# Two batches per unit, zero-padded 128-row matmuls and an MLP interleaved by hand in a sigmoid-attention kernel

## The chip, the cores and the metric

The kernel runs on one core of a Trainium2 chip. The metric is the device time of one execution in microseconds (us), as a median of several runs. Times of single stretches and instructions come from one profiled execution of each kernel. A run counts as slow when it lies over 1.5% above the fastest of the same kernel.

## The reference, cut to what matters

```python
# q, k, v: (8, 12, 448, 64) float32; w_q, w_k: (768, 64); w_out: (768, 768)
scores = q @ k^T / sqrt(64) - log(448)
attn   = 1 / (1 + exp(-scores))              # sigmoid, no row sums
x      = attn @ v                            # heads side by side: (8, 448, 768)
wq, wk = x @ w_q, x @ w_k
W_tok  = wq @ wk^T / sqrt(64)
out    = relu(W_tok @ x) @ w_out
```

There is no softmax, so score tiles are independent of each other. The mixing is computed as wq times (wk^T x), which keeps the inner size at 64.

## The kernel before

One batch at a time, a pair of heads at a time, in blocks of 112 rows (448 = 4 x 112).

```python
for b in range(B):                                     # 8 batches
    for hp in range(H // HPC):                         # 6 head pairs
        # load q, k, v in 256-byte runs, cast, transpose q and k  ... (cut)
        for hh in range(HPC):
            po = hh * HD
            for kb in range(NSB):                      # 4 blocks of 112 keys
                sco = psum.tile([SB, S], F32, tag="p")
                nc.tensor.matmul(sco, kT[po:po+HD, kb*SB:(kb+1)*SB],   # 64 rows of the array
                                 qT[po:po+HD, :], start=True, stop=True)
                attnT = work.tile([SB, S], BF16, tag="attnT")
                nc.scalar.activation(attnT, sco, Sigmoid, bias=bias_t[:SB], scale=attn_scale)
                nc.tensor.matmul(pxt[po:po+HD, :], vsb[:, kb, hh, :],  # 64 columns of the array
                                 attnT, start=(kb == 0), stop=(kb == NSB-1))
    # MLP of this batch, in blocks of 112 rows  ... (cut)
```

The order of the instructions is left to the scheduler. Weights are loaded whole, first of all.

## Time and profile before

| | before |
|---|---|
| median time | 499.0 us (498.6 to 499.98, 4 runs) |
| a batch: attention, MLP | 33.0 us, about 23 to 24 us |
| score tiles | 384 of 112 x 448 |
| mean granted TensorE clock | 0.94 |

In the profile, PE is TensorE (matmuls), PEld its weight loads, DVE VectorE, ACT ScalarE, POOL GpSimd and SPq the queue that issues DMAs; L404 is a line of the kernel. Matmuls write into PSUM, which the kernel's pools take in banks; SBUF is the working memory that the engines read from. The profile's page gives the busy time of each engine, the clock by slices, the chain of work that ended last, and groups of instructions with their mean duration and what ended the engine's idle time before them. The duration of a matmul includes time in the pipeline, in which the next one may already run. What a matmul costs in a stream is the distance between two starts. The prediction below shows the lines.

### The profile page before, as it was taken

How to read it: one execution, taken by the hardware profiler on the slowest of the kernel's cores; microseconds unless marked ns; L12 is line 12 of the kernel's file. 1: busy time of each engine (PE TensorE's matmuls, PEld its weight loads, DVE VectorE, ACT ScalarE, POOL GpSimd, SP SyncE). 2: the span in 40 equal slices, each digit the busy share in tenths (PEclk: the TensorE clock that was granted, in tenths of full speed). 3: DMA queues.
4: the chain of work that ended last, by engine and by line, in shares of the span. 5: the costliest groups of instructions: out<-in, count | busy, mean ns of one | idle time of the engine just before them, and what ended most of it. 6: DMA issues, size and time to landing. Idle time of an engine off the chain costs nothing.

```text
span 497.1 us, 6003 instructions
## 1 busy us (share of the span) xinstructions
PE 467.5 (94%) x2080; PEld 220.4 (44%) x2080; DVE 126.8 (26%) x363; ACT 348.0 (70%) x675; POOL 0.7 (0%) x7
## 2 busy tenths in 40 slices
PE   0699999999999999999999999999999999999986
PEld 0233344643446434643446434643446434553345
DVE  0121122043322431143221421233231432233100
ACT  1856555488856896488866896578865896578963
POOL 0000000000000000000000000000000000000000
PEclk9999999999979999699979999699979999699989
DMA  9634240365525441445325441345325452331003
GB/s 260 146 72 95 57 94 18 91 149 114 117 61 161 106 96 38 114 126 116 71 57 163 99 110 38 100 127 113 86 50 151 100 121 46 80 106 38 0 1 111
DMA packets 144206, 47.19 MB, mean 95 GB/s; under 512 B 136240, under 2 KB 143408, under 8 KB 144176
## 3 DMA queue, kind: packets, MB, share of 16 engines
q1 hardware_dynamic: 144176, 46.82, 38.7%
q8 instruction: 16, 0.26, 0.2%
q14 instruction: 14, 0.11, 0.1%
HBM read 35.78 MB, written 11.01 MB: 94 GB/s over the span
## 4 chain that ended last, share of the span: by engine, by line
PE 92%; ACT 3%; DMA 2%; issue 1%; DVE 0%; SPq 0%; ACTq 0%
PE sco L105 26%; PE pxt L116 25%; PE po L176 15%; PE ptr L94 7%; PE pt L128 6%; PE ptmp L156 4%; PE pm L165 4%; PE pwk L144 2%; DMA wo<-in_moe_w_out_dram 2%; PE pwq L135 2%; ACT x L131 1%; ACT xT L123 1%; ACT wout_sb L59 1%; DVE wk L149 0%; ACT L112 0%
## 5 line engine op out<-in xcount | busy, mean ns | idle before, releaser
L112 ACT ACTIVATE attnT<-sco,bias_t 112x448 bf16<-112x448 f32 x384 | 237.9, 634 | 38.9 <-PE pxt L116 36.1
L105 PE MATMUL sco<-qT,kT 64*112 64x448 bf16 x384 | 153.8, 417 | 1.7 <-ACT kT L98 1.5
L116 PE MATMUL pxt<-attnT,vsb 112*64 112x448 bf16 x384 | 152.2, 402 | 0.7 <-ACT attnT L112 0.7
L105 PEld LDWEIGHTS <-kT 64*112 64x112 bf16 x384 | 48.6, 130 | 80.4 <-issue 75.8
L176 PE MATMUL po<-wout_sb,mixT 128*112 128x384 bf16 x384 | 77.1, 370 | 0.0
L116 PEld LDWEIGHTS <-vsb 112*64 112x64 bf16 x384 | 40.8, 109 | 62.4 <-issue 50.7
L176 PEld LDWEIGHTS <-mixT 128*112 128x112 bf16 x384 | 57.1, 151 | 18.5 <-issue 0.7
L183 ACT COPY osb<-po 112x384 f32<-112x384 f32 x63 | 30.1, 478 | 46.9 <-PE po L176 38.3
L128 PE MATMUL pt<-ident,xT 128*112 128x128 bf16 x192 | 42.8, 260 | 7.4 <-ACT x L131 5.6
L131 ACT COPY x<-pt 112x128 bf16<-112x128 bf16 x119 | 28.4, 266 | 21.3 <-PE pt L128 15.8
L94 PE MATMUL ptr<-ident,qsb 112*128 112x112 bf16 x192 | 29.6, 249 | 14.2 <-DVE qsb L83 14.2
L123 DVE CAST xT<-pxt 128x448 bf16<-128x448 f32 x36 | 22.5, 625 | 77.4 <-PE pxt L116 77.4
L98 DVE COPY kT<-ptr 128x448 bf16<-128x448 bf16 x47 | 18.2, 387 | 85.8 <-PE ptr L94 85.8
L98 DVE COPY qT<-ptr 128x448 bf16<-128x448 bf16 x41 | 16.0, 391 | 68.6 <-PE ptr L94 48.0
L131 DVE COPY x<-pt 112x128 bf16<-112x128 bf16 x73 | 15.4, 223 | 68.2 <-PE pt L128 67.2
L128 PEld LDWEIGHTS <-xT 128*112 128x112 bf16 x192 | 21.7, 141 | 22.4 <-issue 15.5
L94 PEld LDWEIGHTS <-qsb 112*128 112x128 bf16 x192 | 15.3, 114 | 32.5 <-issue 16.8
L94 PE MATMUL ptr<-ident,ksb 112*128 112x112 bf16 x192 | 26.2, 238 | 0.8 <-DVE ksb L83 0.8
L167 ACT ACTIVATE mixT<-pm 128x448 bf16<-128x448 f32 x48 | 22.6, 546 | 5.7 <-PE pm L165 5.7
L156 PE MATMUL ptmp<-x,wk 112*64 112x384 bf16 x64 | 25.9, 404 | 0.3 <-DVE x L131 0.3
L83 DVE CAST vsb<-vsb 112x512 bf16<-112x512 f32 x47 | 19.7, 418 | 24.5 <-PE pxt L116 24.5
L94 PEld LDWEIGHTS <-ksb 112*128 112x128 bf16 x192 | 13.7, 107 | 20.1 <-issue 16.0
(33 smaller groups left out, 163.7 us busy)
## 6 DMA issues: line engine op xcount, KB each, us to landing
qsb<-in_q_dram SPq DMA_DIRECT2D x96, 112.0 KB, 2.7
ksb<-in_k_dram SPq DMA_DIRECT2D x96, 112.0 KB, 2.6
vsb<-in_v_dram SPq DMA_DIRECT2D x96, 112.0 KB, 2.4
out_dram<-osb SPq DMA_DIRECT2D x64, 168.0 KB, 2.2
wo<-in_moe_w_out_dram SPq DMA_DIRECT2D x1, 2304.0 KB, 11.3
wq<-in_moe_w_q_dram SPq DMA_DIRECT2D x1, 192.0 KB, 2.6
wk<-in_moe_w_k_dram SPq DMA_DIRECT2D x1, 192.0 KB, 2.9
```

The source lines that it names most:

```text
L94: nc.tensor.transpose(ptr[:, c * SB:(c + 1) * SB], src[:, c, :, :], ident16[:SB, :SB],)
L98: nc.any.tensor_copy(out=dst, in_=ptr)
L105: nc.tensor.matmul(sco, kT[po:po + HD, kb * SB:(kb + 1) * SB], qT[po:po + HD, :], start=True, stop=True,)
L112: nc.scalar.activation(attnT, sco, mybir.ActivationFunctionType.Sigmoid, bias=bias_t[:SB], scale=attn_scale,)
L116: nc.tensor.matmul(pxt[po:po + HD, :], vsb[:, kb, hh, :], attnT, start=(kb == 0), stop=(kb == NSB - 1),)
L123: nc.any.tensor_copy(out=xT_sb[hp], in_=pxt)
L128: nc.tensor.transpose(pt, xT_sb[c][:, si * SB:(si + 1) * SB], ident16[:DC, :DC])
L131: nc.any.tensor_copy(out=x_sb[si][:, c * DC:(c + 1) * DC], in_=pt)
L156: nc.tensor.matmul(ptmp, wk_s[si], x_sb[si][:, nb * 384:(nb + 1) * 384], start=(si == 0), stop=(si == NSB - 1),)
L167: nc.scalar.activation(mixT[c], pm, mybir.ActivationFunctionType.Relu, bias=0.0, scale=moe_scale,)
L176: nc.tensor.matmul(po, mixT[c][:, si * SB:(si + 1) * SB], wout_sb[:, c, nb * 384:(nb + 1) * 384], start=(c == 0), stop=(c == NDC - 1),)
L183: nc.any.tensor_copy(out=osb, in_=po)
```

## The change

The intent: fill the 128 x 128 array at every matmul, halve the number of sigmoids, stop waiting for weights at the start, and hide the MLP's TensorE work under the attention of the next two batches. The order of instructions on each engine is fixed by hand.

```diff
-    for b in range(B):
-        for hp in range(H // HPC):
+    NI, NP = 7, 64                      # 448 rows = 64 partitions x 7; two batches fill 128
+    kz = [singles.tile([P, NI, P], BF16, name=f"kz{n}") for n in range(NKZ)]       # zero-padded k
+    vz = [[singles.tile([P, NJ, NI, P], BF16, ...) for b in range(2)] for n in range(2)]
+    ps_s = pool("ps_s", 2, ...)         # scores: 2 buffers of 2 banks
+    ps_v = pool("ps_v", 2, ...)         # value accumulators: 2 banks
+    ps_f = pool("ps_f", 2, ...)         # q and k transposes and every MLP tile: 2 banks
+    ctx.enter_context(tc.manual_schedule())
...
+    for n, (u, j) in enumerate(pairs):  # 4 units x 6 head pairs
+        if n == 1:
+            load_weights()              # DMA and POOL casts of all weights, here
+        cast_qk(u1, j1); cast_v(u1, j1); tr = transposes(u1, j1)     # for the next pair
+        if j == 0 and u > 0:
+            fill = mlp(u - 1)
+            per_group = sum(c for c, _ in fill) / (NI * NJ - 2)
+        for gg in range(NI):            # a group: two score tiles
+            for slot in range(2):
+                nc.tensor.matmul(sc[:, slot, 0:S], kzt[u, j, b2][:, kblk, :], qt..., ...)
+            nc.scalar.activation(at, sc[:, :, 0:S], ACTF.Sigmoid, bias=bias_t, scale=attn_scale)
+            for _ in range(3):
+                if tr: tr.pop(0)[1]()   # 7 q transposes, then 7 k transposes
+            if len(pv_q) > LAG: flush_pv()              # value matmuls, two groups late
+            credit += per_group         # then MLP matmuls by an estimated cost
+            while fill and credit >= fill[0][0]:
+                cst, fn = fill.pop(0); credit -= cst; fn()
```

(An eviction is the copy of a PSUM tile to SBUF.) Loads now come in runs of up to 1792 bytes, and the casts from float32 are POOL's.

## The prediction

> **What bounds the kernel now.** I read the page's busy table first, then the clock row, the chain that ended last, the groups, and last two stretches of batch 2 (attention, then MLP) by engine and by instruction.
>
> ```profile
> PE 467.5 (94%) x2080; PEld 220.4 (44%) x2080; DVE 126.8 (26%) x363; ACT 348.0 (70%) x675; POOL 0.7 (0%) x7
> PEclk9999999999979999699979999699979999699989
> PE 92%; ACT 3%; DMA 2%; issue 1%; DVE 0%; SPq 0%; ACTq 0%
> L112 ACT ACTIVATE attnT<-sco,bias_t 112x448 bf16<-112x448 f32 x384 | 237.9, 634 | 38.9 <-PE pxt L116 36.1
> L105 PE MATMUL sco<-qT,kT 64*112 64x448 bf16 x384 | 153.8, 417 | 1.7 <-ACT kT L98 1.5
> L116 PE MATMUL pxt<-attnT,vsb 112*64 112x448 bf16 x384 | 152.2, 402 | 0.7 <-ACT attnT L112 0.7
> L176 PE MATMUL po<-wout_sb,mixT 128*112 128x384 bf16 x384 | 77.1, 370 | 0.0
> ```
>
> TensorE is 94% busy and 92% of the chain, so it sets the time, but busy is not streaming: a matmul's bar is longer than the distance to the next one. The stretches by engine (columns: stretch, length, busy time of PE, weight loads, DVE, ACT, POOL, then clock, DMA share, GB/s) give the period of a batch:
>
> ```profile
> 155.56:188.59 33.03, 33.03 (x137) 13.33 (x138) 12.16 (x33) 29.76 (x49) 0.00 (x0) 1.00 0.47 110
> 188.59:212.56 23.97, 22.95 (x126) 13.85 (x124) 4.07 (x13) 12.53 (x35) 0.00 (x0) 0.79 0.31 81
> ```
>
> A batch is 33.0 us of attention at full clock and about 23 to 24 us of MLP at a lower one (0.79 here, 0.85 in the next batch): 57 us, eight times, plus about 19 us before the first sigmoid and a slow first batch. The timeline of TensorE inside attention shows why attention costs 33 us:
>
> ```profile
> 163.34 0.39 PE L105 MATMUL sco<-qT,kT 64*112 64x448 bf16 x1
> 163.66 0.38 PE L116 MATMUL pxt<-attnT,vsb 112*64 112x448 bf16 x1
> 163.97 0.39 PE L105 MATMUL sco<-qT,kT 64*112 64x448 bf16 x1
> 164.29 0.38 PE L116 MATMUL pxt<-attnT,vsb 112*64 112x448 bf16 x1
> ```
>
> A 64-row score matmul and a 64-column value matmul alternate, and each start is 0.31 to 0.32 us after the last. Matmuls of one full-array shape do much better: consecutive starts of the output matmuls (L176, N=384) lie 0.162 us apart. So a score tile costs TensorE 0.63 us, and 48 tiles 30 us. ACT looks bound too (a 0.634 us sigmoid in a 0.63 us period), but right at the start, where score tiles had queued up behind the table load, five sigmoids take 2.95 us:
>
> ```profile
> 19.44 2.95 ACT L112 ACTIVATE attnT<-sco,bias_t 112x448 bf16<-112x448 f32 x5
> ```
>
> They include a wait; the first four start 0.53, 0.52 and 0.52 us apart. ACT can do a tile in 0.52 us; TensorE can't.
>
> **What the Trainium skill says.** (1) "TensorE: Matmul & The Clock Gate", section "Back-to-back issue gap": warm, N/2.4 + 2.5 ns. That is 162.5 ns at N=384, and the trace has 162; it gives 189 ns at N=448, and the trace has 189 between the wq matmuls (L135, 128 rows by 64 columns, one after another). (2) "TensorEngine Tiling (Array Packing)", section "Key Properties": changing the tiling mode drains the engine. The 0.31 us against 0.189 us above agrees. (3) "Advanced Engine Details and Errata", section "The Read-Write Bubble": each ACT or DVE instruction pays a fixed latency, so use large tiles; several PSUM banks may be read at once. The trace agrees on the fixed part: ACT's copies of 128 and 384 elements take 266 and 478 ns, 0.83 ns an element, so 0.52 us for 448 is 373 ns of elements and some 143 ns fixed. (4) "VectorE: DVE Perf Modes", section "Zero memsets can be issued as uint32 (trn2)": a memset takes a cycle per element whatever the type. No instruction of the kernel before shows it.
>
> **The change part by part.** There are now four units of two batches, six head pairs each, seven groups a pair. A group is two score matmuls, one sigmoid over 2x448, two value matmuls, two transposes on average and a share of the previous unit's MLP.
>
> *Attention on TensorE.* 336 score tiles of 128 rows for 384 of 112, all 128x128 on the array, so no mode switch: 4 x 189 = 756 ns a group, and 14 transposes a pair at 56 ns (128 columns by (1)), 112 a group: 868 ns. For the two batches that is 42 x 0.868 = 36.5 us; it was 66.
>
> *ACT.* By the fixed part of (3) a 2x448 sigmoid should start 143 + 747 = 890 ns after the last: 42 a unit are 37.4 us, plus 12 Relu of 448 at 440 ns (their distance in the trace), 5.3: 43 us a unit. No bound except in unit 0, which has no MLP to fill with.
>
> *MLP.* Per unit 24 matmuls of 448, 98 of 384 and 49 transposes: 4.5 + 15.9 + 2.7 = 23.2 us; it was 2 x 23 to 24. It sits between the attention matmuls at full clock. Streaming sum of a unit with filling: 36.5 + 23.2 = 59.7 us.
>
> *DVE.* A bf16 eviction of 448 takes 391 ns (448/1.92 + 158) but the next starts after 309; fp32 takes 625. A pair: q 625, k in eight pieces about 1.9 us, two value evictions 1.25; a unit with MLP about 40 us. Not a bound, but its queue is in order.
>
> *POOL.* Casts of 2560 elements a pair. From the small POOL rows (a memset of 128 takes 204 ns and of 1 takes 99; the select 292) 0.8 to 1.5 ns each, so some 2 to 4 us and overheads. Hidden under a 6 to 14 us pair.
>
> *Stalls that the hand order adds.* Two PSUM banks (ps_f) serve the q and k transposes and every MLP tile. TensorE is in order. While a transpose tile is open (groups 0 to 4 of 7) the MLP has one bank, so when one MLP tile ends and the next begins within a group, TensorE waits for the tail of the matmul (0.215 us past its stream), DVE (0.558) and two semaphore hops (0.04 + 0.05): **0.87 us**. Going through the written order of a unit, I count per pair: the first k transpose directly after the last q one (also 0.87, while an MLP tile holds the other bank); one or two mid-group boundaries of output tiles; and one tile that must wait behind the eight k evictions (0.4 to 1.5). This is 3.0, 4.2 and 3.2 us in pairs 3 to 5, 1.3 in pair 0, 7.0 in pair 1 (six x transposes a tile). In pair 2 the mix tiles are one matmul each and go through ACT's Relu (about 0.85 us a tile): 7.9. Sum **26.6 us a unit**. Some will overlap or be given back, so I take three quarters: 20. A filled unit is 59.7 + 20 = 80 us.
>
> *Start.* q and k no longer wait for the 2.3 MB weight. But DVE clears 26,880 bf16 columns before its first eviction: 28 us at a cycle each, 14 if issued as uint32. First sigmoid at 18 or 32 us; weight casts may hold up pair 1 somewhat. I take 25.
>
> *Tail.* The last MLP stands alone: 2.3 us of wq/wk, x transposes at DVE's pace with the clock falling (6.5), 3.5, mix at 0.51 us a tile (6.3), output 14.5, last eviction and store 4, the last value group 1: 38 us.
>
> Sum: start 25 + unit 0 at about 0.92 us a group (the first four groups of a pair have three transposes, 924 ns, the rest are ACT's 890) 39 + 3 x 80 + tail 38 = 342. The bank waits are the softest term and I counted them pessimistically, so I settle at **332 us**, 0.67 of before.
>
> **The rivals.** *A: no bank stalls.* If evictions keep pace, a filled unit is 60 to 62 us and the total 275 to 285. For it: an eviction is shorter than a six-matmul tile. Against it: two banks, three kinds of tile, in-order TensorE. *B: stalls in full, and the memset at one cycle per 2-byte element*: 32 + 40 + 3 x 87 + 40 = 373. *C: POOL is the bound.* At 3 ns an element with overheads a pair is 8.5 us, above unit 0's 6.4 but below a filled pair: some 13 us more, about 345. *D: ACT's sigmoid doesn't overlap with the next* (1007 ns a group): unit 0 becomes 43, the filled units stay as they are: 336. *E: the padding buys nothing* and full matmuls still cost 0.31 us: attention alone is 42 x 4 x 0.31 = 52 us a unit and the total near 400; the 0.162 and 0.189 us spacings speak against it. None reaches 499.
>
> **Range and chances.** A and B are the two ends, hence 285 to 375. Faster by over 2%: 0.97; within 2%: 0.02; slower: 0.01, for something like a POOL cast several times slower than its rows suggest.
>
> **What would show it.** Score and value matmuls 0.19 us apart within a group: the mode switch is gone. Sigmoids of about 1.0 us, 0.89 to 0.95 us apart in unit 0. A clock near 1.0 until the tail. Idle or waiting time of TensorE at the first k transpose, the x transposes, the mix and the output tiles, released by DVE evictions or the Relu, of 15 to 27 us a unit: right; under 5 us: rival A. The first sigmoid's time tells the memset. The prediction is wrong if POOL's casts release the transposes in the filled units, or if spacing within a group stays near 0.31 us.

## The result, and the profile after

| | before | after |
|---|---|---|
| median time | 499.0 us | 379.25 us (376.41 to 379.62, 4 runs) |
| ratio | | 0.7588, 95% interval 0.7562 to 0.7615 |
| span of the profiled run | 497.1 us | 377.2 us |

A ratio is the mean time of one kernel's fast runs over that of the other's of the same rounds, so it is not quite the ratio of the medians. The change is a clear gain. The time lies above the predicted 332 us and 4 us outside the range of 285 to 375.

The page of the changed kernel (the rows of busy time, clock, DMA, the chain by engine, then groups as in the prediction: count, busy us, mean ns, idle before and its releaser):

```profile
PE 276.6 (73%) x1692; PEld 149.8 (40%) x1692; DVE 161.6 (43%) x391; ACT 189.3 (50%) x217; POOL 88.4 (23%) x177
...
PEclk9995599999579999999999999999958999999989
DMA  8995999990000137839940039728960011232046
...
PE 55%; DVE 19%; DMA 7%; ACT 6%; SPq 6%; issue 4%; POOL 2%; POOLq 0%
...
L409 ACT ACTIVATE at<-sc,bias_t 128x896 bf16<-128x896 f32 x168 | 164.8, 1009 | 128.5 <-PE sc L404 110.4
L404 PE MATMUL sc<-qt,kz 128*128 128x448 bf16 x336 | 96.7, 371 | 7.6 <-DVE kz L182 6.3
L359 PE MATMUL pv<-at,vz 128*128 128x448 bf16 x336 | 95.5, 368 | 0.0
L271 PE MATMUL po<-wout,mx 128*128 128x384 bf16 x336 | 70.7, 332 | 17.5 <-DVE o L277 10.6
```

TensorE fell from 94% busy to 73% and from 92% of the chain to 55%; DVE (19%), DMA and others have entered it. No engine is busy throughout, which is how a kernel looks that waits. The clock row drops to 5 in three places. The duration of a score matmul hardly changed (417 to 371 ns), so the gain must be looked for in the distance of starts. The timeline of TensorE in unit 0, which has no MLP to interleave (columns: start, length, line, operation, count):

```profile
57.63 0.54 PE L404 MATMUL sc<-qt,kz 128*128 128x448 bf16 x2
58.01 0.33 PE L164 MATMUL ptr<-ident,q 128*128 128x128 bf16 x3
58.18 0.54 PE L359 MATMUL pv<-at,vz 128*128 128x448 bf16 x2
58.55 0.54 PE L404 MATMUL sc<-qt,kz 128*128 128x448 bf16 x2
```

Two score matmuls take 0.38 us of the stream (57.63 to 58.01), three transposes 0.17, two value matmuls 0.37. That is 0.19 us a matmul, where the kernel before needed 0.31 to 0.32. A group lasts 0.92 us here. The sigmoids of 896 elements start 0.89 to 0.92 us apart.

Now the stretches by engine. The rows are unit 0 (from its first sigmoid), units 1, 2 and 3 (3 up to the last sigmoid), and the tail:

```profile
core 0: us, PE busy (x) PEld busy (x) DVE busy (x) ACT busy (x) POOL busy (x), PEclk, DMA share, GB/s
18.20:76.60 58.40, 40.13 (x246) 21.72 (x245) 21.25 (x65) 38.46 (x44) 29.71 (x56) 0.85 0.97 231
76.60:167.60 91.00, 70.18 (x424) 37.77 (x423) 37.40 (x95) 47.83 (x56) 17.16 (x34) 0.92 0.34 82
167.60:254.10 86.50, 65.05 (x426) 35.58 (x423) 37.52 (x96) 47.89 (x55) 20.25 (x40) 1.00 0.52 128
254.10:338.90 84.80, 67.04 (x399) 35.91 (x396) 34.04 (x85) 46.92 (x54) 12.23 (x24) 0.92 0.38 92
338.90:377.20 38.30, 29.92 (x184) 16.24 (x181) 17.29 (x32) 6.93 (x13) 0.00 (x0) 0.96 0.36 91
```

Two batches of attention with an MLP take 84.8 to 91 us where they took 2 x 57 before, though DVE is busy for 34 to 38 us and ACT for 47 of them. Against the sum in the prediction:

| part | predicted | measured |
|---|---|---|
| start, to the first sigmoid | 25 (18 or 32) | 18.2 |
| unit 0 | 39 | 58.4 |
| units 1 to 3 | 240 | 91.0 + 86.5 + 84.8 = 262.3 |
| tail | 38 | 38.3 |
| sum | 342, recorded as 332 | 377.2 |

Three places explain the difference. The first is one pair in unit 0. In the next fence the rows are pairs 1 and 2 of unit 0, then pair 1 of units 1 and 2:

```profile
25.90:51.10 25.20, 8.38 (x46) 4.52 (x47) 3.76 (x12) 6.54 (x8) 15.58 (x28) 0.66 0.90 226
51.10:57.40 6.30, 6.30 (x44) 3.51 (x42) 3.61 (x11) 6.30 (x8) 3.03 (x6) 1.00 1.15 216
87.40:108.60 21.20, 16.22 (x93) 9.00 (x91) 8.21 (x20) 7.05 (x7) 3.03 (x6) 0.68 0.00 1
178.80:195.00 16.20, 10.60 (x89) 6.55 (x88) 8.21 (x20) 7.05 (x7) 6.25 (x13) 1.00 0.84 203
```

Pair 1 of unit 0 lasts 25.2 us, its neighbour 6.3. POOL's timeline tells why (in brackets: idle time before and what ended it):

```profile
27.98 0.51 POOL L333 CAST wqk<-wq 128x384 bf16<-128x384 f32 x1 [10.94 <-DMA wq<-in_moe_w_q_dram]
...
34.09 0.83 POOL L339 CAST wout<-w 128x768 bf16<-128x768 f32 x1 [2.31 <-DMA w<-in_moe_w_out_dram]
...
40.96 0.83 POOL L339 CAST wout<-w 128x768 bf16<-128x768 f32 x1 [2.05 <-DMA w<-in_moe_w_out_dram]
41.73 0.93 POOL L127 CAST q<-q 128x896 bf16<-128x896 f32 x1
```

POOL runs its queue in order. The weight casts stand in it ahead of the q cast of pair 2 and wait for their transfers, which stand behind those of four pairs in a DMA queue that is 0.90 busy over this stretch. The q cast, whose data had long landed, starts at 41.73 us, and TensorE waits 17.0 us for it at once (the longest wait of its transposes for POOL).

The second place is the filled units. The list of waits names what TensorE waited for (total us, times, longest):

```profile
PE pm L259 <- ACT mx L264: 14.1, 23, 0.9
...
PE po L271 <- DVE o L277: 10.6, 14, 1.0
...
PE px L223 <- DVE xn L228: 8.0, 13, 0.7
PE ptr L164 <- DVE qt L171: 7.2, 10, 0.7
```

These are the four costliest of the kinds of tile that share the two banks of `ps_f`: mix, output, x transposes, and k behind q. One such wait in the timeline of pair 3 of unit 2:

```profile
218.68 0.49 PE L271 MATMUL po<-wout,mx 128*128 128x384 bf16 x2
219.21 0.56 DVE L277 COPY o<-po 128x384 f32<-128x384 f32 x1 [2.48 <-PE po L271]
219.82 0.48 PE L271 MATMUL po<-wout,mx 128*128 128x384 bf16 x2 [0.65 <-DVE o L277]
```

The second of the two matmuls at 218.68 starts 0.16 later and ends its stream at about 219.0. The next tile's first matmul, of the same group, starts at 219.82. In between lie the tail of the matmul, an eviction of 0.56 and the hops: about 0.8 us with nothing on TensorE. To add all of them up I took the distance of each two starts on TensorE, less N/2.4 + 2.5 ns at the granted clock, wherever it is more than 0.06 us over. In unit 2, by pair, against the count in the prediction:

| pair | 0 | 1 | 2 | 3 | 4 | 5 | unit |
|---|---|---|---|---|---|---|---|
| counted, us | 1.3 | 7.0 | 7.9 | 3.0 | 4.2 | 3.2 | 26.6 |
| measured, us | 2.0 | 6.9 | 7.0 | 2.9 | 4.4 | 3.5 | 26.7 |

The third place is the clock. Pair 1 of unit 1 ran at 0.68 and took 21.2 us, pair 1 of unit 2 at 1.00 and took 16.2, with the same TensorE work and nearly the same waits (6.2 and 6.9 us). In units 1 and 3 the clock was at half for 13.7 us, in unit 2 never.

### The profile page after: what moved, and what is told of

Same layout as the page of the kernel before. It is cut to its first block, busy times and chain, and to the rows that moved or that the text cites. A ratio compares the mean times of both kernels' runs of the same rounds, so it can differ in the third digit from the quotient of the medians.

```text
span 377.2 us, 4927 instructions
## 1 busy us (share of the span) xinstructions
PE 276.6 (73%) x1692; PEld 149.8 (40%) x1692; DVE 161.6 (43%) x391; ACT 189.3 (50%) x217; POOL 88.4 (23%) x177
## 4 chain that ended last, share of the span: by engine, by line
PE 55%; DVE 19%; DMA 7%; ACT 6%; SPq 6%; issue 4%; POOL 2%; POOLq 0%
PE sc L404 14%; PE pv L359 13%; PE po L271 13%; DVE kz L182 5%; PE ptr L164 5%; ACT mx L264 4%; PE px L223 3%; DMA k<-in_k_dram 3%; PE pt L247 3%; SPq L100 3%; DVE xt L364 2%; PE pm L259 2%; DVE o L277 2%; PE pw L208 2%; DVE xn L228 2%
## 5 line engine op out<-in xcount | busy, mean ns | idle before, releaser
L409 ACT ACTIVATE at<-sc,bias_t 128x896 bf16<-128x896 f32 x168 | 164.8, 1009 | 128.5 <-PE sc L404 110.4
L404 PE MATMUL sc<-qt,kz 128*128 128x448 bf16 x336 | 96.7, 371 | 7.6 <-DVE kz L182 6.3
L359 PE MATMUL pv<-at,vz 128*128 128x448 bf16 x336 | 95.5, 368 | 0.0
L271 PE MATMUL po<-wout,mx 128*128 128x384 bf16 x336 | 70.7, 332 | 17.5 <-DVE o L277 10.6
L364 DVE CAST xt<-pv 128x448 bf16<-128x448 f32 x48 | 30.0, 624 | 64.4 <-PE pv L359 64.1
L182 DVE COPY kz<-ptr 64x384 bf16<-64x384 bf16 x96 | 34.1, 355 | 42.7 <-PE ptr L164 40.3
L277 DVE COPY o<-po 128x384 f32<-128x384 f32 x56 | 31.1, 556 | 48.0 <-PE po L271 44.2
L271 PEld LDWEIGHTS <-mx 128*128 128x128 bf16 x336 | 32.9, 99 | 46.5 <-issue 13.5
L404 PEld LDWEIGHTS <-kz 128*128 128x128 bf16 x336 | 33.1, 101 | 45.4 <-issue 17.9
L138 POOL CAST vz<-v 128x192 bf16<-128x192 f32 x96 | 29.4, 346 | 1.9 <-DMA v<-in_v_dram 1.5
```

What stands on the lines that cost most here:

```text
L138: nc.gpsimd.tensor_copy(out=z[:, j, 3 * hh : 3 * hh + 3, 64 * hh : 64 * hh + 64], in_=t[:, hh].rearrange("p (m d) -> p m d", m=3),)
L182: nc.vector.tensor_copy(out=z[r, 3 * hh : 3 * hh + 3].rearrange("p m (r n) -> p r m n", r=2), in_=ps[r, 0:6, b2].rearrange("p (r m) n -> p ...
L271: nc.tensor.matmul(st["po"], st["mx"][c][:, i * P : (i + 1) * P], wout16[:, c, nb * NB : (nb + 1) * NB], start=(c == 0), stop=(c == NC - 1),)
L277: nc.vector.tensor_copy(out=st["o"][:, nb * NB : (nb + 1) * NB], in_=st["po"])
L359: nc.tensor.matmul(ps, vz[u % 2][b2][:, j, (blk // 2 + 3 * (blk % 2)) if blk < 6 else 6, :], at[:, slot, :], start=(blk == 0), stop=(blk = ...
L364: nc.vector.tensor_copy(out=xts[u][j][:, :, b2, :], in_=ps)
```

## The experiments

All gave correct results. The first four ran on one chip in one set of rounds, the next four in another, the last two in a third; the kernel before took 498.1, 499.2 and 498.6 us there. The changed kernel itself had 379.25 us.

**Weights spread over the pairs.**

```diff
-        if n == 1:
-            load_weights()
         ...
             cast_v(u1, j1)
             tr = transposes(u1, j1)
+        weights_cast(n)    # n == 2: wq, wk; n == 2..4: two chunks of w_out each
+        weights_dma(n)     # n == 1: wq, wk; n == 1..3: two chunks of w_out each
```

> Only the weights move: two chunks a pair, cast behind the pair's own casts, in place of all of them ahead of pair 2's casts. My theory: pair 1 of unit 0 took 25.2 us in place of 6.3 only because POOL, in order, held the q cast of pair 2 behind weight casts that waited for a saturated DMA queue. It expects pair 1 near 7 us, unit 0 near 40 us and a total of 379 - 18 = 361 us (357 to 365). Rival: the first 80 us are bound by the DMA bandwidth itself (0.99 busy), so the same bytes cost the same time wherever they stand: pair 1 gets short, but later pairs of unit 0 get longer, total 374 or more.

Measured: 356.8 us (351.34 to 365.01, 4 runs); two of the runs count as slow, the fast two took 351.34 and 356.03. Pair 1 of unit 0 took 6.3 us and unit 0 39.6:

```profile
26.00:32.30 6.30, 6.30 (x44) 3.52 (x43) 3.62 (x11) 6.30 (x9) 5.00 (x11) 1.00 1.14 283
18.20:57.80 39.60, 38.15 (x241) 20.65 (x239) 21.14 (x65) 38.27 (x43) 24.50 (x45) 1.00 1.09 254
```

All weights were cast by 49 us, between the pairs' own casts, and no later pair of unit 0 became longer than 6.6 us. The theory stands and the bandwidth rival falls: 58.4 - 39.6 = 18.8 us were lost to where the weights stood in the queues. (The edit moves the weights' transfers and their casts together; the two were not tried apart.) The fast runs lie just under the expected 357 to 365 us: in the profiled one the clock was at half in one filled unit in place of two. The last experiment returns to the spread between runs.

**The MLP in one piece, nothing interleaved.**

```diff
-            fill = mlp(u - 1)
-            per_group = sum(c for c, _ in fill) / (NI * NJ - 2)
+            while pv_q:
+                flush_pv()
+            for _, f in mlp(u - 1):
+                f()
```

> The MLP of a unit runs in one piece ahead of the next unit's attention, nothing interleaved. My theory: two PSUM banks make the interleaving cost about as much as it hides. Attention alone is 42 groups of 0.9 us = 38 us (as in unit 0), the MLP alone about 33 us (as in the tail), with the restart some 72.5 us a unit, against 86 to 91 interleaved: total about 333 us (325 to 345). Rival: interleaving does hide work, as it was meant to, and taking it away makes each of three units longer: 380 us or more.

Measured: 321.39 us (319.75 to 324.08, 4 runs). Taking the interleaving away made the kernel 58 us faster. The theory was right in direction and too cautious by 12 us. The two rows are the last pair of unit 0 with the MLP behind it, and the first pair of attention after that:

```profile
69.40:106.80 37.40, 33.26 (x218) 18.61 (x217) 19.60 (x41) 12.35 (x20) 3.03 (x6) 1.00 0.23 57
106.80:113.10 6.30, 5.86 (x42) 3.21 (x39) 3.24 (x11) 6.26 (x8) 0.35 (x1) 1.00 0.89 236
```

The MLP alone takes 37.4 - 6.3 = 31.1 us and six pairs of attention 37.8, so 68.9 us a unit against 84.8 to 91 interleaved. In one piece the MLP has both banks, and the waits of a unit add up to 9.3 us by the measure above.

**One whole MLP tile a group.**

```diff
-                credit += per_group
-                while fill and credit >= fill[0][0]:
-                    cst, fn = fill.pop(0)
-                    credit -= cst
-                    fn()
+                for fn in fill.pop(0)[1]:   # fill now lists tiles: 38 for 40 groups
+                    fn()
```

> The MLP is cut at tile ends: one whole tile a group (38 tiles, 40 groups), so that the attention matmuls of a group stand between two tiles. Same instructions, same banks. My theory: the 26.6 us a filled unit are waits for a bank between two MLP tiles in one group; most of them go, what stays is the first k transpose (about 5 us a unit) and waits behind the k evictions (2 to 3 us), and the mix groups become ACT's (3.6 us more). A filled unit near 71 us, total about 329 us (320 to 342). Rival: the evictions on DVE are the limit whatever the order, so the waits move but stay: 365 us or more.

Measured: 316.05 us (314.52 to 317.01, 4 runs), below the expected band. The waits of a filled unit fell from 26.7 to 8.1 us and the unit to 68.0 (unit 2, where the changed kernel took 86.5 at the same clock):

```profile
144.70:212.70 68.00, 62.77 (x425) 35.45 (x424) 37.00 (x95) 46.00 (x56) 20.30 (x40) 1.00 0.63 163
```

The DVE rival falls: every eviction is still there and takes as long. The mix groups did not become as long as I had feared (I had added 3.6 us), and the clock stayed at 1.0 in all filled units.

**A third bank for the filling pool.**

```diff
-    ps_v = pool("ps_v", 2, space=bass.MemoryType.PSUM)
-    ps_f = pool("ps_f", 2, space=bass.MemoryType.PSUM)
+    ps_v = pool("ps_v", 1, space=bass.MemoryType.PSUM)
+    ps_f = pool("ps_f", 3, space=bass.MemoryType.PSUM)
```

> A bank goes from the value accumulators (2 to 1) to the filling pool (2 to 3), order unchanged. My theory: about 20 of the 26.6 us a filled unit go; each pair pays 0.9 us where the second batch's accumulation begins right behind the first one's (about 5.5 us a unit, and 5 to 8 in unit 0, which has no slack). Total about 342 us (330 to 358), waits at the first value matmul released by the DVE eviction of the value accumulator. Rival: the number of banks in the filling pool is not what TensorE waits for; then only the cost shows: 395 us or more.

Measured: 343.37 us (342.54 to 345.33, 4 runs). In the list of waits a new first entry for TensorE stands, the price foretold:

```profile
PE pv L359 <- DVE xt L364: 37.9, 31, 2.0
```

The waits for the filling pool fell from 26.7 to about 5 us a unit (mix 3.3, k transposes 1.4, x 0.5), and the value accumulators added 10.4, more than the 5.5 that I had estimated. Without touching the order, the number of banks alone moves the waits. That is the direct proof of what TensorE waited for. That the total met the estimate is in part luck: the price was higher than estimated, in unit 0 too (67.6 us for 58.4), and the clock, at half for only 3.4 us in the filled units against 27 in the changed kernel, gave some 9 us back.

**k transposes later, on top of one tile a group.**

```diff
             for _ in range(3):
-                if tr:
+                if tr and (gg >= 3 or len(tr) > NI):
                     tr.pop(0)[1]()
```

> The one-tile-a-group kernel (316 us), and the seven k transposes start in group 3 in place of right behind the last q transpose. My theory: the first k transpose waits for the bank that q's eviction frees; in the one-tile kernel the starts of transposes lag 2.7 us a filled unit behind the stream. Most of that goes: 310 us (306 to 313). Rival: the k evictions now end too late for the next pair's first scores, and each of 23 pairs pays for it: 320 us or more.

Measured: 308.4 us (307.99 to 308.73, 4 runs). The starts of transposes now lag 0.4 us a filled unit in place of 2.7, and a unit takes 65.5 us. The first scores of a pair still find their k in time. The theory stands.

**Score matmuls without the padding of k.**

```diff
+                r = slice(0, P) if blk == 6 else slice(64 * (blk % 2), 64 * (blk % 2) + 64)
                 nc.tensor.matmul(
-                    sc[:, slot, 0:S], kzt[u, j, b2][:, kblk, :],
-                    qt[u, j][:, b2].rearrange("p i n -> p (i n)"), start=True, stop=True,
+                    sc[:, slot, 0:S], kzt[u, j, b2][r, kblk, :],
+                    qt[u, j][r, b2].rearrange("p i n -> p (i n)"), start=True, stop=True,
```

> The changed kernel, but six of seven score matmuls of a batch take only the 64 rows that hold data (no zero padding of k in use); their two row halves alternate. My theory: going from 64 rows to 128 and back drains the array, 0.126 us each time as in the kernel before (0.315 against 0.189 us a start), so a group costs 0.25 us more, a pair of unit 0 goes from 6.3 to 7.8 or 8 us and the total to about 420 us (405 to 430). Rival: the two halves run side by side on different rows, the second starting some ns after the first, which pays for the drains: pair of unit 0 6.3 to 6.7 us, total 376 to 390.

Measured: 394.05 us (389.12 to 398.86, 4 runs); two of the runs count as slow (mean clock 0.887), the fast two took 389.12 and 389.72. By these the total lies inside the rival's band and below mine. The timeline of TensorE in unit 0 shows what happens inside a group:

```profile
60.44 0.36 PE L405 MATMUL sc<-qt,kz 64*128 64x448 bf16 x2
60.74 0.29 PE L164 MATMUL ptr<-ident,k 128*128 128x128 bf16 x2
60.86 0.54 PE L359 MATMUL pv<-at,vz 128*128 128x448 bf16 x2
```

Two score matmuls on different row halves together last 0.36 us, no longer than one alone: their starts in the trace are 0.003 us apart. The first of them starts 0.285 us after the value matmul ahead of it, in place of 0.189, and the next full-array instruction 0.29 after them. So the pair costs about 0.39 us where two padded ones cost 0.38. The rival is right about the mechanism, and about the pairs of unit 0 (6.6 us, against 6.3). Unit 2, at full clock in both kernels, takes 89.2 us against 86.5. At 0.3 us in the pairs of unit 0 and 2.7 in each of three filled units, padding k is worth some 10 us, which is what the fast runs differ by (389 and 379).

The traces also show what the change of mode costs. In a stream of full-array matmuls, the weights of the next one load while the one before runs: in the changed kernel a weight load starts at 57.633 us for the matmul that starts at 57.820. At a change they load only with their own matmul (60.438 and 60.442 here, and so for the alternating score and value matmuls of the kernel before). In that kernel the starts lie 0.118 us over 0.189 (medians) after a value matmul and 0.134 after a score matmul, whose own weight loads take 0.106 and 0.123 us. So its 0.31 us is close to a weight load and a stream one after the other. What holds the load back is not shown.

**One sigmoid per score tile.**

```diff
-            nc.scalar.activation(at, sc[:, :, 0:S], ACTF.Sigmoid, bias=bias_t, scale=attn_scale)
+            for slot in range(2):
+                nc.scalar.activation(at[:, slot], sc[:, slot, 0:S], ACTF.Sigmoid,
+                                     bias=bias_t, scale=attn_scale)
```

> The changed kernel with one sigmoid per score tile (448) in place of one per two (896). My theory: an activation pays 0.14 us whatever its size, so a group of unit 0 takes 1.03 us of ACT in place of 0.90 and a pair 7.2 us in place of 6.3; the filled units stay, TensorE sets them; total about 384 us (380 to 390). Rival: ACT never limits and the finer grain starts value matmuls sooner: no change or less, pairs of unit 0 at 6.3 us or below.

Measured: 378.63 us (376.76 to 384.14, 4 runs; the run of 384.14 counts as slow, the fast three took 376.76 to 378.76). In unit 0 a pair took 7.2 to 7.5 us in place of 6.3 to 6.6, as the theory said: sigmoids start 0.516 us apart, two of them 1.03 us. The total doesn't tell, because the profiled run lost half clock for 17 us where the changed kernel's had lost 27 us in its filled units. The double sigmoid is worth about 1 us in each pair in which ACT sets the pace, and no worth is seen in the filled units (13.0, 14.4 and 14.3 us in pairs 3 to 5 of unit 1, as in the changed kernel).

**The three repairs together.** Spread weights, one tile a group, late k transposes.

> Weights spread over pairs, one MLP tile a group, late k transposes, together. My theory: the gains add, as they lie in different stretches: 316 - 18.5 - 6 = 291 us (286 to 298), unit 0 at 39 us, filled units at 66 us, tail 37. Rival: with unit 0 fast, its loads and those of unit 1 meet a saturated DMA queue and unit 1 gives part of it back: 303 us or more.

Measured: 292.16 us (291.22 to 292.75, 4 runs), ratio to the kernel before 0.5849 (0.5832 to 0.5867). The gains add. This version beats both kernels. Its page, and a filled unit (unit 2):

```profile
PE 257.9 (89%) x1692; PEld 143.6 (49%) x1692; DVE 159.9 (55%) x391; ACT 182.9 (63%) x217; POOL 89.1 (31%) x177
...
PEclk9999999999999999999999999999999999999799
```

```profile
123.70:189.30 65.60, 62.69 (x426) 35.27 (x424) 36.97 (x97) 45.80 (x56) 20.30 (x40) 1.00 0.68 169
```

TensorE is busy for 62.7 of 65.6 us, with 59.7 us of streaming. The clock row has no dip before the tail.

**The MLP in one piece, with spread weights.** The edits of the first two experiments together.

> MLP in one piece and weights spread, no interleaving. What is interleaving worth once its waits are cut? My theory: 321 us less the 18.5 us of the weight hold: 303 us (299 to 307), so well-cut interleaving (292 us) is worth about 10 us over none, far from the 23 us of MLP streaming a unit that it was to hide, because TensorE streams 60 us a unit either way and only the idle time is at stake. Rival: with the pairs at ACT's pace and no slack, loads run late without the MLP's pauses, total 310 us or more.

Measured: 303.99 us (302.72 to 307.1, 4 runs). Well-cut interleaving is worth 304 - 292 = 12 us over none. (The 292 us kernel also has the late k transposes and this one has not; but the waits of most pairs without filling add up to 0.2 us here, so they can explain little of it.) Loads did not run late (no pair of attention over 6.6 us except the first, 8.6).

**x transposes cut at tile ends, with spread weights.**

```diff
                 credit += per_group
+                done = 0
                 while fill and credit >= fill[0][0]:
-                    cst, fn = fill.pop(0)
+                    if fill[0][2] and done:       # an x tile would begin here
+                        credit = 0.0
+                        break
+                    cst, fn, _ = fill.pop(0)
                     credit -= cst
+                    done += 1
                     fn()
```

> The kernel with spread weights, and of the MLP only the x transposes are cut at tile ends (no x tile begins in a group that has already done filling work). Four runs of the spread-weights kernel lay between 351 and 365 us, and its profiled run had TensorE's clock at half for 14 us in the x phase of one of three units, which made that pair 20.8 in place of 16.5 us. My theory: the bank waits in the x phase leave TensorE so idle that the clock falls in some units of some runs; with about 3 us of waits a unit gone it stays up: 343 us (338 to 348), spread between runs under 4 us, clock 1.0 in every unit's x phase. Rival: the transposes as such let the clock fall, not the waits: the spread stays near 10 us and some x phases still show half clock.

Measured: 329.9 us (328.52 to 330.6, 5 runs), a spread of 2 us, and clock 1.0 in all x phases of the profiled run. Of the spread that the run was to explain, 351 to 365 us, the upper two runs count as slow. The fast two lie 4.7 us apart, about what one stretch of half clock costs (20.8 against 16.5 us in pair 1), and their mean clocks agree with that: 0.994 and 0.975, where all five runs here have 0.994 to 0.999. The rival, that transposes as such let the clock fall, is weakened: the same transposes ran at clock 1.0 here, and in the profiled runs of the MLP in one piece, where they stand closer still. It is not excluded: other runs of the latter with spread weights have mean clocks down to 0.982, and where the clock fell in them is not on record. The time is 13 us better than I expected. Setting the credit to zero also moved later tile ends: all waits of a filled unit fell to about 20 us, not only those of the x tiles. So the run shows that the clock stays up when the filling is cut differently; how idle TensorE has to be for it to fall stays open.

## Why the prediction was wrong

Its direction and most of its steps held, and the time came out 47 us above it. In the order of its working:

- **What bounds the kernel before** held. The start distance in attention went from 0.31 to 0.19 us with full-array matmuls. The experiment without k's padding qualifies the reason: a change of mode costs about 0.1 us, with a weight load that no longer overlaps, and two row halves side by side can pay for it. In the kernel before, a 64-row and a 64-column matmul alternated singly, so every start paid. How much of the 0.31 us is due to the value matmul's 64 columns was not tried.
- **The spacing formula**, point (1) from the skill, held: 0.189 us at 448 columns, 0.162 at 384, 0.056 at 128. But that section gives the formula for an isolated matmul and says that a stream with weight loads has other spacings (about 81 ns at N=128, 131 at N=512), which the prediction left out. The trace decides for the formula at 128, and its 448 columns already take longer than those 131 ns; 512 was not run.
- **ACT** held: 0.89 to 0.92 us a sigmoid, unit 0 at 6.3 us a pair, and one sigmoid per tile cost what the fixed part says. Rival D (1007 ns a group) falls with it.
- **Start**: 18.2 us, the lower of the two cases. The memsets are issued as uint32 (2688 elements for 5376). I had taken 25 because I could not tell, and to cover the weight casts.
- **"weight casts may hold up pair 1 somewhat"** is the first step that failed. The mechanism was seen and its size was not worked out: 18.9 us in pair 1, against at most 7 in the sum. The parts were there: six chunks, two buffers, each waiting for a transfer behind four pairs of prefetched loads, and an in-order POOL.
- **The count of the bank waits** held to 0.1 us a unit and to 1 us in each pair.
- **"Some will overlap or be given back, so I take three quarters"** is the step that failed most. Nothing was given back: of the 26.6 us counted, 26.7 stand between the starts of unit 2, at full clock, so each wait of the engine that sets the time was paid in full. The discount took 6.6 us from each of three units, and settling on 332 below the own sum of 342 took 10 more.
- **Clock near 1.0 until the tail** failed too. Units 1 and 3 each lost some 5 us in pair 1 (21.2 and 21.1 against 16.2 us). Why there and not in unit 2 stays open.
- **Tail** held: 38.3 us for 38. Its parts are off by up to 1.2 us in both directions, and the clock fell at the start of the output matmuls (357.0 to 360.4 us), not in the x transposes.

Rival B had the stalls right with 3 x 87 us, and its memset wrong; that its 373 us come so near is luck, as 14 us of a memset that did not happen stand in for the weight casts. Rival C, POOL's rate, was not the bound (a q cast takes 0.94 us), but POOL's order was. A and E fell. The difference to the record, 377.2 - 332 = 45 us by the span, is made of -7 at the start, +19 in unit 0, +22 in the filled units and +10 of the last rounding down.

Where did the rest of the expected gain go? Interleaving was to hide some 23 us of MLP streaming a unit. It cannot, as TensorE streams both: 59.7 us a unit whichever way. Only the idle time beside it can be won, 9.3 us a unit when the MLP stands alone, and cutting by estimated cost spent 27 us of waits to win it.

## What to carry to other kernels

When work is interleaved by hand on an in-order engine, cut it where its buffers change hands: two kernels with the same instructions and banks differ by 63 us (379 and 316), some 10 of them through the clock, and what was changed is only where a group's share of that work ends. Before putting a queue's rare work (weight casts) ahead of its regular work, count what it waits for, because everything behind it waits too. And a wait that has been counted on the path that sets the end should be left at full size in the sum, unless a reason for a discount can be named.

## What the Trainium skill lacked or had wrong

- "TensorEngine Tiling (Array Packing)", section "Key Properties": that a change of mode drains the engine fits the traces, but no size is given there. Here a change between full-array and 64-row matmuls of 448 columns added about 0.1 us (0.285 in place of 0.189 us).
- "TensorE: Matmul & The Clock Gate", Part 1: it has the clock fall to half after an idle window of about 3.4 us. In the changed kernel it fell for 13.7 us in two of three units although TensorE's longest idle time in the 10 us before (84 to 94 us) was 0.92 us. The same part's remark on micro-idling between groups fits better, but gives no threshold, and the runs here don't either.
- "GPSIMD Engine Reference", section "Engine selection": one-input work at roughly line rate agrees (casts of 192 and 896 elements took 346 and 940 ns, 0.84 ns an element; VectorE's copies of 384 and 448 float32 took 556 and 624 ns, 1.06 an element), but the page gives no figure for the fixed part of a cast, here some 0.18 us.
- "VectorE: DVE Perf Modes", section "Zero memsets can be issued as uint32 (trn2)": agrees. Memsets of 2688 words start 2.81 us apart, though each one's row in the profile reads only 2.30 us; that section doesn't warn of it.
